# Holding the q attention of a two-layer transformer kernel to a fixed lead over the GLU blocks

## The chip, the cores and the metric

The kernel runs on one core of a Trainium2 chip. A core has five engines that run their own instruction streams and meet at semaphores: TensorE (PE, with its weight loads shown as PEld), VectorE (DVE), ScalarE (ACT), GpSimd (POOL) and SyncE (SP), which in this kernel only issues DMA transfers. The metric is the device time of one execution in microseconds, taken as the median of several runs.

## The reference

The input is 2048 tokens of width 576. Two layers follow each other with the same weights. Each layer adds a linear attention and then a gated unit (GLU) to the residual x, both on a normalised x:

```
x = x + _A_ref(_layernorm(x, axis=-1), A_wqkv, A_w_phi, A_wo)
x = x + _B_ref(_layernorm(x, axis=-1), B_w_gate, B_w_up, B_w_down)

# attention, 32 heads of 18
phi_q = concatenate([softmax(pq), softmax(-pq)])        # pq = q @ w_phi, per head; phi_k likewise
kv  = einsum("bhsf,bhsd->bhfd", phi_k, v)               # sums over ALL tokens
z   = sum of phi_k over the tokens
o   = (phi_q @ kv) / (phi_q @ z + 1e-6),  then o @ wo

# GLU, 4608 hidden columns
h = (x @ w_gate) * (x @ w_up),  then h @ w_down
```

The k side sums over all tokens, so the q side of a layer cannot finish anywhere before the k side has seen every token. After that, each token's q attention and GLU need only that token's data.

## The kernel before, in words

**Tiles and blocks.** The 2048 tokens are 16 tiles of 128 (`NS`), taken in 8 blocks of two tiles (`NB`). The products w_qkv x w_phi for q and k are folded once at the start. The features of phi (2 x 576 = 1152) are handled as nine blocks of 128 (`NK = 9`), so that one DMA transpose turns a tile's phi into nine 128x128 pieces.

**One q tile (`t_aout`).** Ten matmuls with Wq (five per half of 288 columns, L845) go to two PSUM banks. ACT copies them to SBUF (L858), DVE takes maxima and minima (L861, L866), POOL and DVE subtract them (L871, L880), ACT takes exponentials (L888, L890), DVE sums (L895), ACT forms the reciprocal of the sum (L899, L903), and POOL multiplies twice (L909). Lines 849 to 912 are this softmax front. SP then issues the DMA transpose eT<-dd (L1018). Twelve matmuls eT x BD (L1034, called "num" below) give numerators and denominators, DVE divides (L1041 to L1050), SP issues the transpose oT<-o (L1068), ten matmuls with Wo follow (L845 again), and DVE adds the result to x (L1075). When a block's x is complete, its layer norm (`t_ln`) ends in two DMA transposes xT<-xln (L830), which the GLU reads.

**One GLU block (`t_bmain`, `t_down`).** First come 648 matmuls with gate and up weights (L1115). Behind them ACT copies the gate half (L1158) and DVE multiplies (L1160). While they run, the block holds a lock: no other work may take a PSUM bank. Then come 144 down matmuls, 72 of 512 columns (L1182) and 72 of 64 columns (L1185), over 36 chunks of hidden columns. The down weights are not kept: they are loaded again for each block, two chunks (288 KB) at a time, into four slots `wdr` (L1090), on the same SP queue as all transposes. A slot's load can go out once the matmuls on that slot are done.

**k and v of the next layer.** After a GLU block of layer 1 is finished, its two tiles run the k softmax, v and the kv sum of layer 2 (`t_ain`, `t_kv`: matmuls with Wk, Wv and L940).

**What sets the order.** All of this is written as generators ("threads") for a planner (`Sched`, lines 246 to 457). It keeps an estimated time for each engine, takes the request that can start earliest (with a bonus for some priorities), and appends it to its engine's stream. The order of each engine's instructions, SP's included, is thus fixed when the kernel is built; on the chip, each engine takes its own stream in order and waits only for the data and buffers that it needs. An event such as `("x2", L, b)` (GLU block b of layer L is done) orders threads in the planner alone; no wait on the chip comes from it.

**Where the change acts.** `t_q` (line 1224) starts the q attention of a layer, block by block:

```
for b in range(NB):
    yield ("wait", ("xT", L, b))
    if b >= s.pace[L - 1]:
        yield ("wait", ("x2", L, b - s.pace[L - 1]))
    ...
    for j in range(2):
        yield ("go", s.t_aout(L, 2 * b + j), ...)
    ...
    if s.qdeep[L - 1]:
        yield ("wait", ("qf", L, 2 * b + 1))
```

With `pace = (8, 8)` and eight blocks the inner wait is never reached. A second rule works the other way: from block 1 on, GLU block b is not started before the q attention of block b + 1 is finished (`ahead`, line 1313, for `pol = (0, 0)`).

Of the kernel before, what the change touches and what calls it, by code (L numbers as in the profile page):

```python
# [17 lines left out]
class Tracker:  # L18
    def __init__(self):
        self.ops = {e: [] for e in ENGINES}  # L20
        self.count = {e: 0 for e in ENGINES}
        self.know = {e: {} for e in ENGINES}
        self.snap = {}
        self.fin = {}
        self.lastw = {}
        self.readers = {}
        self.lastacc = {}
        self.dma_groups = []
        self.pend_w = {}
        self.pend_r = {}  # L30
        self.stats = {"ops": 0, "waits": 0, "multiwait": 0, "pe_multiwait": 0}
# [479 lines left out]
class K:  # L511
    def __init__(self, nc, A_x, A_wqkv, A_w_phi, A_wo, B_w_gate, B_w_up, B_w_down, out):
        self.nc = nc
        self.A_x, self.A_wqkv, self.A_w_phi, self.A_wo = A_x, A_wqkv, A_w_phi, A_wo
        self.wg, self.wu, self.wd, self.out = B_w_gate, B_w_up, B_w_down, out
        self.NPS, self.NSM, self.NVX, self.NET, self.NXP, self.NWD, self.NG, self.NO, self.NOT = 2, 4, 2, 2, 2, 4, 2, 1, 2
        self.early = 2
        self.qlead = 4
        self.alt = 1.2
        self.lnlead = 9  # L520
        self.pol0 = 1
        self.qdeep = (1, 1)
        self.pol = (0, 0)
        self.pace = (8, 8)
        self.bias = {10: 300.0, 11: 800.0}
        self.tr = Tracker()
        self.sc = Sched(self.tr)
        self.stack = ExitStack()
# [873 lines left out]
```

## Time and profile before

| | |
|---|---|
| median of 3 runs | 1220.92 us (1220.49 to 1225.0) |
| the profiled execution, its own time | 1221.51 us |
| its span, from first to last instruction | 1219.7 us |
| PE busy | 1107.8 us (91%), mean granted clock 0.969 |
| DVE busy | 597.2 us (49%) |
| ACT busy | 390.6 us (32%) |
| POOL busy | 265.0 us (22%) |
| DMA packets of the dynamic queue | 40.2% of 16 engines' span |

The profile is one execution. Its page gives busy times, a chain of work followed back from the last instruction, and groups of instructions with what ended the idle time before them. Other views list the chain in order of time, single stretches of time with each engine's busy time and the granted TensorE clock, and the timeline of one engine. Ends of matmuls are modelled, so the distance between the starts of neighbouring matmuls, not their length, is their cost.

The span divides by PE's work: 0 to 132.3 us is start and the k side of layer 1, and then each layer has eight GLU blocks. A block's gate and up matmuls (L1115) take about 35.5 us. Between them and those of the next block lies a stretch with the down matmuls and with all attention work. These stretches are numbered by layer and block: stretch 1.0 follows the gate and up matmuls of layer 1, block 0, and stretch 2.7 is the last.

### The profile page before, as it was taken

What the parts mean: (1) busy time and instruction counts of PE and PEld (TensorE: products, weight loads), DVE (VectorE), ACT (ScalarE), POOL (GpSimd) and SP (SyncE); (2) the same over time, 40 slices, a digit from 0 to 9 for tenths busy, and PEclk for the clock granted to TensorE, in tenths of its full rate; (3) what the DMA queues carried; (4) which work ended last, traced back from release to release, by engine and by line L of the source; (5) the groups of instructions that cost most, each with busy time, mean ns of one, the idle gap of its engine ahead of it and who ended that gap; (6) DMA issues with size and microseconds to landing.
All of it is one profiled execution on the core that took longest, in us unless ns stands there. A gap on an engine that the chain in (4) does not pass through costs nothing.

```text
span 1219.7 us, 32683 instructions
## 1 busy us (share of the span) xinstructions
PE 1107.8 (91%) x14738; PEld 833.4 (68%) x14806; DVE 597.2 (49%) x1209; ACT 390.6 (32%) x919; POOL 265.0 (22%) x258
## 2 busy tenths in 40 slices
PE   5875898999999999999999589999989999999998
PEld 4553675868768585858586367686766867768684
DVE  7777557384674434343435655737554312223131
ACT  6664433343433232323234343333331212112120
POOL 5674214142250202020203320504221000000000
PEclk9897899999999999999999789999999999999999
DMA  7473119155381605150504211917437152332414
GB/s 178 89 298 96 19 49 212 29 147 108 81 184 13 191 13 175 14 169 21 167 21 145 51 21 41 225 21 194 90 84 177 32 156 69 118 103 85 147 41 146
DMA packets 182949, 128.59 MB, mean 105 GB/s; under 512 B 101530, under 2 KB 181658, under 8 KB 181658
## 3 DMA queue, kind: packets, MB, share of 16 engines
q1 hardware_dynamic: 182810, 126.51, 40.2%
q8 instruction: 115, 1.88, 0.6%
q14 instruction: 24, 0.20, 0.0%
HBM read 100.59 MB, written 2.36 MB: 84 GB/s over the span
## 4 chain that ended last, share of the span: by engine, by line
PE 72%; DMA 15%; DVE 7%; ACT 3%; POOL 1%; issue 1%; SPq 0%; DVEq 0%
PE ps L1115 47%; DMA wdr<-in_B_w_down_dram 11%; PE ps L1182 10%; PE ps L845 10%; DMA oT<-o 3%; PE ps L1185 2%; PE ps L940 1%; POOL dd L909 1%; DVE ss L895 1%; PE ps L1034 1%; DVE st L790 1%; DVE mxmn L866 1%; DVE mxmn L861 1%; ACT dd L888 1%; DVE o L1050 1%
## 5 line engine op out<-in xcount | busy, mean ns | idle before, releaser
L1115 PE MATMUL ps<-xT,Wu 64*128 64x256 bf16 x4608 | 573.4, 270 | 1.2 <-DVE x_sb L1206 0.9
L1115 PE MATMUL ps<-xT,Wg 64*128 64x256 bf16 x4608 | 573.0, 270 | 1.6 <-ACT xT L826 1.6
L1115 PEld LDWEIGHTS ps<-xT,Wg 64*128 64x128 bf16 x4608 | 431.3, 95 | 34.1 <-issue 2.6
L1115 PEld LDWEIGHTS ps<-xT,Wu 64*128 64x128 bf16 x4608 | 434.1, 95 | 29.9 <-DVE x_sb L1206 1.3
L1160 DVE TENSOR_TENSOR hT<-ps,gsb 128x512 bf16<-128x512 f32 x288 | 198.8, 691 | 343.3 <-ACT gsb L1158 342.9
L1158 ACT CAST gsb<-ps 128x512 bf16<-128x512 f32 x288 | 168.4, 585 | 527.4 <-PE ps L1115 526.6
L1182 PE MATMUL ps<-wdr,hT 128*128 128x512 bf16 x1084 | 295.3, 383 | 26.3 <-DMA wdr<-in_B_w_down_dram 25.4
L1182 PEld LDWEIGHTS ps<-wdr,hT 128*128 128x128 bf16 x1152 | 112.8, 98 | 170.2 <-DMA wdr<-in_B_w_down_dram 51.5
L1185 PE MATMUL ps<-wdr,hT 128*128 128x64 bf16 x1152 | 222.6, 193 | 4.6 <-issue 0.8
L1115 PE MATMUL ps<-xT,Wr 64*128 64x256 bf16 x1152 | 171.8, 271 | 0.0
L909 POOL TENSOR_TENSOR dd<-dd,ss 128x576 bf16<-128x576 bf16 x123 | 141.2, 1172 | 137.7 <-ACT ss L903 137.7
L871 POOL TENSOR_TENSOR dd<-psb,mxmn 128x576 bf16<-128x576 bf16 x62 | 72.9, 1180 | 388.9 <-DVE mxmn L861 388.9
L1185 PEld LDWEIGHTS ps<-wdr,hT 128*128 128x128 bf16 x1152 | 113.2, 98 | 1.3
L895 DVE TENSOR_REDUCE ss<-dd 128x64 f32<-128x1152 bf16 x64 | 85.4, 1341 | 32.0 <-ACT dd L890 31.8
L1206 DVE TENSOR_TENSOR x_sb<-ps,x_sb 128x512 bf16<-128x512 f32 x32 | 21.7, 679 | 128.6 <-PE ps L1185 128.6
L812 POOL TENSOR_SCALAR xln<-x_sb,nmean,rstd 128x576 bf16<-128x576 bf16 x59 | 47.9, 820 | 146.3 <-ACT rstd L808 146.3
L1115 PEld LDWEIGHTS ps<-xT,Wr 64*128 64x128 bf16 x1152 | 68.6, 95 | 7.2
L858 ACT CAST psb<-ps 128x288 bf16<-128x288 f32 x128 | 50.0, 396 | 61.1 <-PE ps L845 60.3
L888 ACT ACTIVATE dd<-dd 128x576 bf16<-128x576 bf16 x64 | 43.6, 681 | 63.0 <-DVE dd L880 62.9
L845 PE MATMUL ps<-Wo,oT 128*128 128x288 bf16 x320 | 51.0, 297 | 10.7 <-DMA oT<-o 7.9
L861 DVE TENSOR_REDUCE mxmn<-psb 128x32 f32<-128x576 bf16 x64 | 47.6, 743 | 25.4 <-ACT psb L858 25.4
L845 PE MATMUL ps<-Wv,xT 128*128 128x288 bf16 x320 | 55.0, 307 | 3.7 <-ACT vx L925 2.6
(71 smaller groups left out, 793.1 us busy)
## 6 DMA issues: line engine op xcount, KB each, us to landing
wdr<-in_B_w_down_dram SPq DMA_DIRECT2D x288, 288.0 KB, 3.3
Wg<-in_B_w_gate_dram SPq DMA_DIRECT2D x4, 1152.0 KB, 12.6
Wu<-in_B_w_up_dram SPq DMA_DIRECT2D x4, 1152.0 KB, 14.9
x_sb<-in_A_x_dram SPq DMA_DIRECT2D x8, 288.0 KB, 3.3
out_dram<-x_sb SPq DMA_DIRECT2D x8, 288.0 KB, 3.2
Wraw<-in_A_wqkv_dram SPq DMA_DIRECT2D x8, 144.0 KB, 2.9
xT<-xln SPq DMA_TRANSPOSE x58, 3.1
Wv<-in_A_wqkv_dram SPq DMA_DIRECT2D x1, 576.0 KB, 4.2
```

What stands on the lines that cost most here:

```text
L845: ops.append(Op(d_pe(n), (lambda e, lhsT=lhsT, rhs=rhs, k=k: e.matmul(s.ps[:, bank, 0:n], lhsT, rhs, start=(k == 0), stop=(k == 4))), read ...
L858: yield ("ops", "act", [Op(d_actc(288), (lambda e, h=h, bank=bank: e.copy(psb[:, pz, 288 * h:288 * h + 288], s.ps[:, bank, 0:288])), reads ...
L861: ops = [Op(665, (lambda e: e.tensor_reduce(mxmn[:, pz, 0, :], p3, AX.X, ALU.max)), reads=[("psb", pz, 0), ("psb", pz, 1)], writes=[("mx", ...
L871: yield ("alt", [(eng, [Op(dur, (lambda e: e.tensor_tensor(d1, p3, mxb, ALU.subtract)), reads=[("psb", pz, 0), ("psb", pz, 1), ("mx", pz)] ...
L888: yield ("ops", "act", [Op(590, (lambda e: e.activation(de2, de2, ACTF.Exp, scale=-1.0)), reads=s.ddk(sm, 1), writes=s.ddk(sm, 1))])
L895: Op(1320, (lambda e: e.tensor_reduce(ss[:, sm, :].rearrange("p (b g) -> p b g", b=2), e4, AX.X, ALU.add)), reads=s.ddk(sm, 0) + s.ddk(sm, ...
L909: yield ("alt", [(eng, [Op(dur, (lambda e, ev=ev, rb=rb: e.tensor_tensor(ev, ev, rb, ALU.mult)), reads=s.ddk(sm, br) + [("ss", sm)], write ...
L1115: out.append(Op(54.3, (lambda e, bank=bank, cs=cs, lhsT=lhsT, rhs=rhs, st=st, sp=sp: e.matmul(ps[:, bank, cs], lhsT, rhs, start=st, stop=s ...
L1158: yield ("ops", "act", [Op(540, (lambda e, g=g, gb=gb: e.copy(gsb[:, g, :], ps[:, gb, :])), reads=[("gu", gb)], writes=[("gsb", g)], excl= ...
L1160: yield ("ops", "dve", [Op(625, (lambda e, g=g, ub=ub, p=p: e.tensor_tensor(hT[:, p, :], ps[:, ub, :], gsb[:, g, :], ALU.mult)), reads=[(" ...
L1182: ops.append(Op(d_pe(512), (lambda e, lhsT=lhsT, bank=bank, slot=slot, fi=fi, f=f: e.matmul(ps[:, bank, 0:512], lhsT, s.wdr[:, slot, fi, 0 ...
L1185: ops.append(Op(d_pe(64) + 3, (lambda e, lhsT=lhsT, sl=sl, slot=slot, fi=fi, f=f: e.matmul(ps[:, Z, 64 * sl:64 * sl + 64], lhsT, s.wdr[:, ...
```

## The change

One line: the lead of q attention over finished GLU blocks is limited to 4 blocks in layer 1 and 3 in layer 2.

```diff
@@ -521,7 +521,7 @@
         self.pol0 = 1
         self.qdeep = (1, 1)
         self.pol = (0, 0)
-        self.pace = (8, 8)
+        self.pace = (4, 3)
         self.bias = {10: 300.0, 11: 800.0}
         self.tr = Tracker()
         self.sc = Sched(self.tr)
```

q attention of block b in layer 1 now starts, in the planner, when GLU block b - 4 is done, and in layer 2 when GLU block b - 3 is done. No instruction is added or removed on any engine; their order on all five changes. Matmuls in each stretch, in the order that the two programs have (Wq, Wk, Wv, Wo are L845; num is L1034; kv is L940; all stretches also have the 144 down matmuls):

| stretch | before | after |
|---|---|---|
| 1.0 | num 60, Wq 50, Wo 40 | num 60, Wq 40, Wo 40 |
| 1.1 | Wo 40, num 36, Wq 30, Wk 20, Wv 20, kv 20 | Wo 40, num 36, Wq 20, Wk 20, Wv 20, kv 20 |
| 1.2 | num 60, Wq 40, Wo 40, Wk 20, Wv 20, kv 20 | Wq 20, num 24, Wo 20, Wk 20, Wv 20, kv 20 |
| 1.3 | Wo 20, num 12, Wk 20, Wv 20, kv 20 | the same as 1.2 |
| 1.4 | Wk 20, Wv 20, kv 20 | the same as 1.2 |
| 1.5, 1.6, 1.7 | | as before |
| 2.0 | num 60, Wq 50, Wo 40 | num 48, Wq 20, Wo 40 |
| 2.1 | Wo 45, num 60, Wq 50 | Wq 40, num 24, Wo 20 |
| 2.2 | Wo 55, num 48, Wq 20 | num 24, Wo 20 |
| 2.3 | none | Wq 40, num 24, Wo 20 |
| 2.4 | none | num 24, Wo 20 |
| 2.5 | none | Wq 20, num 24, Wo 20 |
| 2.6, 2.7 | none | none |

In the changed program, PE's order inside the new stretches is (down counts single matmuls):

```
1.2, 1.3, 1.4:  Wq20 down32 Wk5 Wv5 down4 Wk10 Wv5 Wk5 down4 Wv5 down20 Wv5 down8 num12 down20 num12 down16 kv6 Wo5 kv8 Wo5 kv6 down16 Wo5 down4 Wo5 down20
2.1, 2.3:       Wq20 down96 num12 down8 num12 down32 Wo5 down4 Wo5 down4 Wq20 Wo10
2.2, 2.4:       num12 down16 num12 down20 Wo5 down4 Wo5 down16 Wo5 down4 Wo5 down84
```

and SP's order of loads (w) and transposes, where loads of slots 1 to 4 of a stretch have gone out in the stretch before:

```
1.2, 1.3, 1.4:  w5 eT w1 eT w4 oT w3 oT w5 (xT x4 later, beside the gate and up matmuls)
2.1, 2.3:       w8 eT w1 eT w4 oT w4 oT w1 out (xT x2, and eT x2 of the second pair, beside the gate and up matmuls)
2.2, 2.4:       w1 oT w3 oT w8 xT xT w6 out
```

## The prediction

> **What bounds the kernel now.** I read the page's chain first, then the groups, then single stretches. The chain and the costliest down group:
>
> ```profile
> PE 72%; DMA 15%; DVE 7%; ACT 3%; POOL 1%; issue 1%; SPq 0%; DVEq 0%
> ...
> L1182 PE MATMUL ps<-wdr,hT 128*128 128x512 bf16 x1084 | 295.3, 383 | 26.3 <-DMA wdr<-in_B_w_down_dram 25.4
> L1182 PEld LDWEIGHTS ps<-wdr,hT 128*128 128x128 bf16 x1152 | 112.8, 98 | 170.2 <-DMA wdr<-in_B_w_down_dram 51.5
> ```
>
> PE carries the end, and where it does not, a load of down weights does. The same PE work is done after the change, so only PE's idle time and its clock can move. They lie in the stretches between the gate and up matmuls. I asked for these one by one (start:end, then length, then busy time and instructions of PE, PEld, DVE, ACT, POOL, clock, DMA share, GB/s):
>
> ```profile
> 171.10:207.40 36.30, 32.94 (x289) 20.73 (x294) 28.00 (x70) 12.15 (x31) 16.15 (x15) 1.00 0.78 186
> 243.51:279.92 36.41, 34.88 (x305) 22.65 (x310) 30.34 (x71) 15.46 (x43) 18.82 (x18) 1.00 0.64 163
> 315.47:356.64 41.17, 37.37 (x338) 24.88 (x344) 34.60 (x82) 17.15 (x45) 22.06 (x20) 1.00 0.73 169
> 392.19:422.95 30.76, 27.72 (x234) 16.47 (x238) 14.62 (x33) 7.86 (x21) 8.48 (x8) 1.00 0.59 168
> 458.49:485.15 26.66, 24.36 (x202) 13.98 (x206) 10.30 (x18) 7.11 (x17) 6.89 (x6) 1.00 0.58 171
> ...
> 751.10:786.14 35.04, 33.06 (x289) 20.80 (x294) 27.45 (x68) 12.15 (x31) 15.88 (x15) 1.00 0.78 192
> 822.70:859.60 36.90, 32.98 (x294) 21.11 (x299) 29.17 (x74) 13.01 (x35) 16.82 (x16) 1.00 0.85 189
> 895.24:934.41 39.17, 33.36 (x263) 19.83 (x267) 20.85 (x57) 7.37 (x21) 10.10 (x10) 0.91 0.79 178
> 970.00:990.83 20.83, 18.45 (x142) 8.92 (x144) 1.36 (x3) 0.58 (x1) 0.00 (x0) 1.00 0.77 226
> ```
>
> These are stretches 1.0 to 1.4 and 2.0 to 2.3. Even 2.3, with nothing but down matmuls, is not full. The timeline prices PE's work by distance of starts: a pair of down matmuls 0.245 us (402.40 to 402.64), five projections 0.614 (394.61 to 395.22), twelve num 0.62, twenty kv 1.2. So 72 pairs are 17.64 us, and 2.3 holds 3.2 us of **remainder** (length less work). By the same prices the remainders are, from 1.0 to 1.6: 4.5, 2.2, 4.5, 3.9, 2.9, 2.4, 2.0 (22.4 in all), and from 2.0 to 2.6: 3.2, 4.5, 9.8, 3.2, 3.2, 3.2, 2.4 (29.5).
>
> 2.2 stands out. SP's timeline and the chain in order of time show why:
>
> ```profile
> 904.79 3.16 SPq L830 DMA_TRANSPOSE xT<-xln  x2
> 907.99 1.09 SPq L1090 DMA_DIRECT2D wdr<-in_B_w_down_dram  x2
> ...
> 908.62 3.65 DMA wdr<-in_B_w_down_dram
> ```
>
> Two xT transposes, ready only at 904.79, stood ahead of two loads whose slots were free. PE then sat idle for 2.6 us, and the record has PE at half clock for some 3.4 us from 912.2 and again from 929.2 (mean 0.91 in the row above). That is 6.4 us of idle and 3.4 us of lost clock.
>
> **What the skill says.** The Trainium skill, DMA: Bandwidth & Descriptors, "Anatomy of one DMA", has any semaphore wait happen on the issuing sequencer; so one late transpose holds every load behind it. The rows above agree. Its fit there, 2.0 us + bytes/436e3, gives 2.7 us for 288 KB; the trace's median is 3.3, which I use. TensorE: Matmul & The Clock Gate, "Back-to-back issue gap", gives N/2.4 + 2.5 ns: 216 for 512 columns and 29 for 64, in sum 245, as traced. The same page, "What's actually happening", halves the clock after an idle window of about 3.4 us. The trace differs: 2.6 us and 2.2 us of idle were enough, while 2.1 us before 858.9 and 1.7 us before 352.7 were not. So I price idle over 2.2 us in one place at another 1.7 us, half of the time.
>
> **The change part by part.** Nothing is added or removed, and the new condition orders only the planner. No new wait exists on the chip. What changes is the place of each piece, and what stands behind what.
>
> *Layer 1, stretches 1.0 and 1.1.* Each loses ten Wq (1.23 us). 1.0 keeps its other pattern: 36.3 to 35.1. 1.1 has 33.0 us of work and now a longer bare run of down matmuls; with 3.2 of remainder it is 36.2 (before 36.4).
>
> *1.2, 1.3, 1.4.* Each has 80 projections (9.82), num 24 (1.24), kv (1.2) and down (17.64), together 29.9 us. For the remainder I followed one by hand. The first tile's Wq ends at 1.4 us. From there to its eT transpose the trace shows 8.5 to 15.0 us over the tiles in GLU stretches: 12.5 and 13.0 for the pair at 316 us, which k work follows as here, and 15.0 and 14.7 for the pair at 263 us, which is mixed with it. I take 12.5: issue at 13.9. The transpose takes 3.6 to land: 17.5. PE reaches this num after 68 down matmuls and twelve groups of five projections, at 15.9, so it waits 1.6. Then the second eT stands ahead of slot 11's load, and that load comes 1.3 us late. The earlier load holes are filled by Wk and Wv. With slot 10 (0.2) and 0.6 for changing between kinds of matmul (what 2.3 has above the same reckoning) that is 3.7. So 33.6 each, 100.8 for three, against 41.2 + 30.8 + 26.7 = 98.7 before: +2.1. In all layer 1 gives -1.2 - 0.2 + 2.1 = **+0.7**.
>
> *Layer 2, 2.0.* 27.5 us of work and the old 3.2: 30.7 (before 35.0), -4.3.
>
> *2.1 and 2.3.* 60 projections, num 24, down: 26.3 us. The first pair at 751 us, with the same start, issued its eT at 764.62 and 766.36, 13.5 and 15.3 after the stretch began; without the num ahead of it I take 13.0 and 14.7. The 96 down matmuls and two load holes of 0.6 end at 15.6; eT lands at 16.6: 1.0. Slot 13's load stands behind the first eT and slot 14's behind the second: 0.7 and 0.4. With the holes (1.1) and 0.6 for changes the remainder is 3.8: 30.1 each.
>
> *2.2 and 2.4.* 20 projections, num 24, down: 21.3 us. Their q front runs beside the gate and up matmuls, so eT is there at the start. But two xT transposes stand ahead of slot 17. The last Wo ends near 13 us, and in the trace 5.2 to 6.1 us pass from the last addition to x (L1075) to xT; with two issues of 1.25 slot 17 leaves near 21 and lands near 24.5. PE waits about 2.3 there, plus 0.7 at oT, 1.1 at two loads, 0.6: 26.0 each.
>
> *2.5* 23.8 + 3.8: 27.6. *2.6* is as before.
>
> Sum of layer 2: 30.7 - 35.0, 30.1 - 36.9, 26.0 - 39.2, 30.1 - 20.8, 26.0 - 20.9, 27.6 - 20.9 = -4.3 - 6.8 - 13.2 + 9.3 + 5.1 + 6.7 = **-3.2**.
>
> *Gate and up matmuls.* Where Wq groups come just ahead of them, ACT and DVE still have a front to run: 36.6 us after 2.0 before, 35.6 elsewhere. The last Wq group now lies ahead of two such blocks (after 2.1 and 2.3) with two tiles, and no longer ahead of that one. I add 1.0 each and take off 1.2: +0.8; the cover is PSUM's three rotating bank pairs, and without it a whole front on DVE (4.4 us for two tiles) would be the loss. For clock, 2.3 us of idle in 2.2 and 2.4 is at the border: 2 x 1.7 x half = +1.7.
>
> Total: 0.7 - 3.2 + 0.8 + 1.7 = **0.0 us**. The sum is against the profiled execution, 1221.51 (span 1219.7 and 1.8 around it), 0.6 above the median of the runs, 1220.92. I forecast a median of 1221 us, that is, no change.
>
> **The rivals.** A change within 0.5% (6.1 us) can't be told from none.
>
> *Slower: eT comes late in the new stretches.* In seven of them (1.1 to 1.4, 2.1, 2.3, 2.5) the first num and the loads behind the eT wait for a front through ACT, DVE and POOL. For: POOL takes its pieces in order (1.17 us each, seven or more ahead), and the trace has 14.7 to 15.0 us beside k work. Against: 10.3 to 12.1 for pairs alone. Each us beyond what I took is one us per stretch, as no other PE work stands ready. With 15 in four and 13.5 in three it is 4 x 2.5 + 3 x 1.9 = +16, with a clock drop in some: 1237. It decides from 0.9 us late on average (seven stretches, 6.1 us).
>
> *Faster: the spread fills the load holes.* For: 1.4 to 1.6, which have attention and no q front, leave 2.0 to 2.9. If all new stretches left 2.2, layer 1 would gain 3 x 1.5 + 1.0 = 5.5 and layer 2 another 3 x 1.6 + 2 x 2.5 = 9.8, and no clock would drop (1.7): 17 in all, 1204. At half of that, where every new stretch has the 3.2 of bare down matmuls, it is 1212. It decides from 0.7 us less in each of nine. Against: the new 2.1 and 2.3 run 96 down matmuls bare, and the trace has no stretch with a q front below 2.2.
>
> That the change does nothing is excluded: the order differs on all five engines.
>
> **How the numbers follow.** No change 0.45, slower 0.33 (hand reckonings leave out waits for banks and for busy engines, which only add), faster 0.22. The likeliest one's own range is 1215 to 1227. Eight in ten reaches to half of the fast case and to nearly the whole slow one: 1211 to 1236.
>
> **What would show it.** 2.2 at clock 1.00 or shorter than 27 us shows the healed part. 2.1 and 2.3 near 30 and 1.2 to 1.4 near 33 show the remainders; over 32 and 35, with waits for eT and for loads behind it, show the slow rival; under 28.5 and 32, the fast one. The gate and up matmuls after 2.1 and 2.3 should be near 36.6. I am wrong if a clock drop turns up in several new stretches, or if planner and chip disagree on when fronts are ready.

## The result, and the profile after

The changed kernel took 1230.41 us (median of four runs, 1229.0 to 1230.75) against 1222.78 (four runs beside it, 1220.49 to 1225.0): 1.006 of the time before, with a 95% interval of 1.0035 to 1.0086. A second set of runs later gave 1.0051 (1.0033 to 1.0068). So the change costs 0.5 to 0.6%, some 6.1 to 7.6 us. The forecast was 1221, no change; its range, 1211 to 1236, holds the time, but the narrower 1215 to 1227 given for "no change" does not.

The profiled execution of after has a span of 1228.5 us (own time 1230.18), 8.8 above the 1219.7 of before. Its page has the chain and the costliest down group as follows:

```profile
PE 73%; DMA 16%; DVE 4%; ACT 3%; POOL 2%; issue 1%; SPq 0%; DVEq 0%
...
L1182 PE MATMUL ps<-wdr,hT 128*128 128x512 bf16 x1152 | 310.2, 385 | 32.1 <-DMA wdr<-in_B_w_down_dram 31.2
L1182 PEld LDWEIGHTS ps<-wdr,hT 128*128 128x128 bf16 x1152 | 113.5, 98 | 176.2 <-DMA wdr<-in_B_w_down_dram 55.8
```

DMA's share of the chain is one point higher, and the idle time that ends with a load of down weights went from 25.4 to 31.2 us. (The count rises to 1152 because the trace of before lacks some matmul records, not because there is more work.) The view of PE's waits says it more directly. It lists, over the whole span, what PE waited for: us in total, number of times, longest. First before, then after:

```profile
PE ps L1182 <- DMA wdr<-in_B_w_down_dram: 25.4, 46, 2.6
...
PE ps L845 <- DMA oT<-o: 7.9, 10, 2.1
PE ps L1034 <- DMA eT<-dd: 6.7, 1, 6.7
```

```profile
PE ps L1182 <- DMA wdr<-in_B_w_down_dram: 31.2, 48, 2.4
...
PE ps L1034 <- DMA eT<-dd: 10.8, 5, 6.7
PE ps L845 <- DMA oT<-o: 8.2, 9, 2.5
```

Loads cost 5.8 us more and eT transposes 4.1 more. All three rows are transfers that SP issues. (These are single executions: a second profile of the changed kernel, `after_rep`, has 28.8 us of waits for loads and 11.3 for eT.) Where they stand is read from the stretches: 1.0 to 1.4, then 2.0 to 2.5 of after (start:end, length, then busy time and instructions of PE, PEld, DVE, ACT, POOL, then clock, DMA share, GB/s):

```profile
170.54:206.48 35.94, 31.96 (x286) 19.70 (x286) 27.33 (x70) 11.89 (x32) 15.42 (x15) 1.00 0.75 186
242.02:284.04 42.02, 35.59 (x301) 22.54 (x300) 27.21 (x65) 12.94 (x36) 15.72 (x15) 0.96 0.66 142
319.59:351.45 31.86, 30.52 (x269) 19.20 (x270) 23.14 (x50) 11.64 (x30) 13.63 (x12) 1.00 0.66 173
386.99:418.90 31.91, 30.52 (x269) 19.17 (x269) 22.94 (x50) 11.64 (x30) 13.63 (x12) 1.00 0.69 173
454.44:488.90 34.46, 32.08 (x270) 20.01 (x270) 23.28 (x50) 11.63 (x30) 13.63 (x12) 0.95 0.67 161
...
754.67:789.40 34.73, 30.24 (x253) 17.79 (x253) 19.75 (x53) 6.44 (x17) 8.49 (x8) 0.95 0.79 182
824.94:855.15 30.21, 27.36 (x230) 15.82 (x228) 15.45 (x35) 7.21 (x17) 8.02 (x7) 1.00 0.85 217
890.70:916.16 25.46, 22.71 (x190) 12.03 (x190) 7.73 (x23) 1.41 (x5) 1.63 (x2) 1.00 0.81 215
951.70:981.56 29.86, 28.15 (x228) 15.88 (x229) 14.82 (x33) 7.20 (x17) 7.33 (x7) 1.00 0.85 220
1017.20:1044.71 27.51, 24.05 (x189) 12.58 (x190) 7.95 (x23) 1.42 (x5) 1.63 (x2) 0.94 0.83 204
1080.27:1110.46 30.19, 25.64 (x209) 14.06 (x210) 13.98 (x31) 5.61 (x13) 6.86 (x6) 0.99 0.86 217
```

2.2 is healed (25.5 at full clock, before 39.2 at 0.91). But five other stretches now contain or begin 3.4 us of half clock: 1.1, 1.4, 2.0, 2.4 and, at its very end, 2.5. Against before:

| | before | forecast | after | what PE waited for in after (us idle) |
|---|---|---|---|---|
| 1.0 | 36.3 | 35.1 | 35.9 | |
| **1.1** | 36.4 | 36.2 | **42.0** | eT 1.8, load 1.6, oT 2.5; half clock |
| 1.2, 1.3 | 41.2, 30.8 | 33.6 each | 31.9, 31.9 | |
| 1.4 | 26.7 | 33.6 | 34.5 | load 2.1; half clock |
| 1.5, 1.6 | 26.2, 25.8 | as before | 26.7, 26.8 | |
| **2.0** | 35.0 | 30.7 | **34.7** | load 2.4; half clock |
| 2.1, 2.3 | 36.9, 20.8 | 30.1 each | 30.2, 29.9 | |
| 2.2, 2.4 | 39.2, 20.9 | 26.0 each | 25.5, 27.5 | in 2.4 load 2.4; half clock |
| **2.5** | 20.9 | 27.6 | **30.2** | eT 1.4, oT 2.3; half clock behind it |
| 2.6 | 20.0 | as before | 20.4 | |
| sum, layer 1 (1.0 to 1.6) | 223.2 | +0.7 | 229.6 | **+6.4** |
| sum, layer 2 (2.0 to 2.6) | 193.7 | -3.2 | 198.4 | **+4.7** |

The rest of the bridge: the gate and up matmuls are 0.6 shorter in layer 1, and those of block 2.0 are 2.5 shorter, because spells of half clock at the border of the layers fell elsewhere. 6.4 + 4.7 - 0.6 - 2.5 is 8.0 and leaves 0.8 for all other parts: 8.8.

**Stretch 1.1, followed.** POOL's timeline and SP's (start, us, operation, names, count):

```profile
255.49 1.63 POOL L812 TENSOR_SCALAR xln<-x_sb,nmean,rstd 128x576 bf16<-128x576 bf16 x2 [5.56 <-ACT rstd L808]
257.08 4.53 POOL L909 TENSOR_TENSOR dd<-dd,ss 128x576 bf16<-128x576 bf16 x4
```

```profile
257.97 2.53 SPq L830 DMA_TRANSPOSE xT<-xln  x2
260.54 2.95 SPq L1018 DMA_TRANSPOSE eT<-dd  x2
263.54 2.14 SPq L1090 DMA_DIRECT2D wdr<-in_B_w_down_dram  x4
```

The layer norm of block 3 (xln) stands ahead of the softmax's last multiplications on POOL, and its two xT transposes ahead of the two eT on SP. Behind all four stand four loads in a row; the first of them, the one that PE waits for, left 4.6 us after its slot came free. (Lateness of a load is counted here from the last matmul on its slot, less the delay of the quickest loads.) From the tile's last Wq to its eT issue pass 15.1 us; in 1.2 to 1.4, without a norm in between, 10.5. The chain in order of time shows the end of it:

```profile
263.54 3.07 DMA wdr<-in_B_w_down_dram
266.61 0.05 issue
266.65 0.61 PE ps L1182
267.26 0.05 PE ps L1185
...
273.28 5.47 DMA oT<-o
278.75 0.04 issue
278.79 0.79 PE ps L845 x5
```

After 1.8 us of waiting for eT and 1.6 for the load, a pair of down matmuls takes 0.61 + 0.05 and the ones behind it 0.48, where 0.245 is the full-clock price. Then an oT transpose takes 5.5 us to land (median of the 28: 3.4), and PE waits 2.5 more.

**Stretch 2.4.** SP's timeline, then the chain:

```profile
1034.03 2.52 SPq L830 DMA_TRANSPOSE xT<-xln  x2
1036.60 6.66 SPq L1090 DMA_DIRECT2D wdr<-in_B_w_down_dram  x5
```

```profile
1036.60 4.39 DMA wdr<-in_B_w_down_dram
1040.99 0.05 issue
...
1041.90 0.43 PE ps L1182
1042.32 0.05 PE ps L1185
```

Again two xT stand ahead of a load, as in 2.2 before: it left 1.4 us after its slot was free, and landed 4.4 us after its issue (median 3.4). Both parts count. Stretch 2.2 of after has the same order of instructions on PE and SP as 2.4; its load behind the two xT left 1.6 us late, but landed in 3.2 us, and PE waited 1.3 us without a drop of the clock. In 1.4 and 2.0 the loads that PE waited for left 1.7 and 1.0 us late, each behind a single transpose (eT, oT), and took 4.9 and 4.8 us to land. So of these waits a part is order on the SP queue and a part slow landing. Among the loads of after with a transpose in flight beside them 18% took over 4.3 us, among the others 11%; what makes a load land late is not shown.

### The profile page after: what moved, and what is told of

Same layout as the page of the kernel before. It is cut to its first block, busy times and chain, and to the rows that moved or that the text cites. A ratio compares the mean times of both kernels' runs of the same rounds, so it can differ in the third digit from the quotient of the medians.

```text
span 1228.5 us, 32776 instructions
## 1 busy us (share of the span) xinstructions
PE 1111.2 (90%) x14806; PEld 833.7 (68%) x14806; DVE 604.0 (49%) x1209; ACT 389.7 (32%) x919; POOL 265.2 (22%) x258
## 3 DMA queue, kind: packets, MB, share of 16 engines
q1 hardware_dynamic: 182810, 126.51, 41.2%
## 4 chain that ended last, share of the span: by engine, by line
PE 73%; DMA 16%; DVE 4%; ACT 3%; POOL 2%; issue 1%; SPq 0%; DVEq 0%
PE ps L1115 46%; PE ps L1182 12%; DMA wdr<-in_B_w_down_dram 11%; PE ps L845 10%; DMA oT<-o 3%; POOL dd L909 2%; PE ps L1185 2%; PE ps L940 1%; PE ps L1034 1%; DVE ss L895 1%; DMA eT<-dd 1%; ACT dd L888 1%; ACT dd L890 1%; DVE mxmn L866 0%; DVE mxmn L861 0%
## 5 line engine op out<-in xcount | busy, mean ns | idle before, releaser
L1182 PE MATMUL ps<-wdr,hT 128*128 128x512 bf16 x1152 | 310.2, 385 | 32.1 <-DMA wdr<-in_B_w_down_dram 31.2
L1115 PE MATMUL ps<-xT,Wr 64*128 64x256 bf16 x1152 | 162.9, 271 | 0.0
L1115 PEld LDWEIGHTS ps<-xT,Wr 64*128 64x128 bf16 x1152 | 61.2, 95 | 6.9
L861 DVE TENSOR_REDUCE mxmn<-psb 128x32 f32<-128x576 bf16 x64 | 47.7, 745 | 27.8 <-ACT psb L858 27.5
L845 PE MATMUL ps<-Wo,oT 128*128 128x288 bf16 x320 | 50.4, 296 | 10.6 <-DMA oT<-o 8.2
L845 PE MATMUL ps<-Wv,xT 128*128 128x288 bf16 x320 | 54.6, 305 | 4.6 <-ACT vx L925 3.5
```

Source lines behind the costliest of these rows:

```text
L845: ops.append(Op(d_pe(n), (lambda e, lhsT=lhsT, rhs=rhs, k=k: e.matmul(s.ps[:, bank, 0:n], lhsT, rhs, start=(k == 0), stop=(k == 4))), read ...
L1115: out.append(Op(54.3, (lambda e, bank=bank, cs=cs, lhsT=lhsT, rhs=rhs, st=st, sp=sp: e.matmul(ps[:, bank, cs], lhsT, rhs, start=st, stop=s ...
L1182: ops.append(Op(d_pe(512), (lambda e, lhsT=lhsT, bank=bank, slot=slot, fi=fi, f=f: e.matmul(ps[:, bank, 0:512], lhsT, s.wdr[:, slot, fi, 0 ...
```

## The experiments

Theory A, formed from the traces: the loss is made on the SP queue. New pairings of transposes and loads make PE wait for loads, eT and oT, and where a wait is long the clock halves on top. Rival B: the loss comes from PE's new order itself (fewer matmuls standing ready while a front runs), and would be there without any load. Rival C: nearly all of it is clock. (In the recorded expectations "theory B" stands for a loss spread over all new stretches, with no such place, and "theory D" for the cost of the q chain itself or of transposes that come late.)

### Each half of the change alone

```diff
-        self.pace = (4, 3)
+        self.pace = (4, 8)   # layer 1 alone; layer 2 alone: (8, 3)
```

> pace = (4, 8): the layer 1 half of the change alone. Its orders in stretches 1.0 to 1.7 are those of the changed kernel, those of 2.0 to 2.7 are those of the kernel before. Theory A (the loss sits in the stretches where the new order begins, above all 1.1, through transposes ahead of loads on SP and the clock drops that follow): stretch 1.1 near 42 us against 36.4 before, 1.0 to 1.6 together near 229 us against 223; time before + 4 to 8 us, 1227 to 1231. Theory B (the loss is spread over all new stretches alike): 1.1 near 38, the three of 1.2 to 1.4 each 1 to 2 us above 32, time before + 3.

> pace = (8, 3): the layer 2 half alone. Theory A: 2.2 shortened from 39 to about 26 us with the clock at 1.00, but 2.0 at 33 to 35 instead of 35, and 2.3 to 2.5 longer by 25 us in sum, as work moved there; time before + 0 to 5 us, 1222 to 1227, depending on how many clock drops fall. Theory B: before + 5 or more. A part of what the changed kernel gained at the start of layer 2 (2.5 us in the gate and up matmuls of block 2.0) would stay or go with where the clock's windows fall, not with this edit.

Layer 1 alone: 1.0023 of before (1.0009 to 1.0036), 2.9 us where theory A had expected 4 to 8. Layer 2 alone: 1.0035 (1.002 to 1.005). The sum, 0.58%, is what the whole change costs. Each half repeats its stretches: with layer 1 alone 1.1 is 41.1 and 1.4 is 34.4, both with half clock, while 2.2 stays at 40.0; with layer 2 alone 1.1 is 36.2, 2.2 is 25.2, 2.0 is 33.8 and 2.5 is 30.3. So the loss comes from both halves, and the forecast's split by layers (+0.7 and -3.2) failed in both, in layer 2 in sign.

### The same kernel again

> The changed kernel once more, beside the others of this call, for a narrower interval: 5 to 8 us above the kernel before. In the trace, stretch 1.1 again near 42 us or, without a clock drop, near 40; 2.0 again 33 to 35; drops of the clock at other places than in the first profile, since their windows lie elsewhere in each execution.

1.0051 (1.0033 to 1.0068). 1.1 was 40.3, 1.4 34.3, 2.4 26.8, 2.5 30.0, all four with half clock again; 2.0 was 33.4 without. So, against the expectation, most places of half clock belong to the program; whether a given wait tips the clock varies. In 2.2 and 2.4, with one order of instructions, the picture is as in after: the loads left 1.4 us late in both, and landed in 3.0 and 4.3 us.

### Filling the waits

At seven waits of the changed kernel (in 1.1, 1.4, 2.0, 2.4 and 2.5) PE gets 62 extra matmuls whose results nobody uses; at the two waits of 2.2 the kernel before gets 20. The one for down matmuls:

```diff
-        ops = []
+        ops = [Op(0.0, (lambda e: e.matmul(ps[:, Z, 128:512], s.ident[:], s.Wo[:, 0, 0:384], start=False, stop=False, ...)), ...)
+               for _ in range(s.fdown.get((L, b, f), 0))]
```

> The changed kernel with 62 extra matmuls (nothing waits for them, their results are not read) on PE just ahead of the seven instructions that PE waited for longest, 1.0 to 1.6 us of work at each, so that PE is busy through most of these waits. The orders of all other instructions stay. If the half clock after idle is a cause of its own (theory A): no clock drop inside 1.0 to 2.6 at these places, and the time falls by 1.7 us for each of the five drops, to 1221 to 1225. If the drops are only company of the idle and cost nothing more (theory C): 1230 or more, up to 1235 if the extra work isn't hidden.

> The kernel before with 20 extra matmuls ahead of the two instructions of stretch 2.2 that waited 2.6 and 2.2 us for loads. Theory A: the two drops go, 2.2 falls from 39.2 to about 36 us, the time by about 3 us, to 1218 to 1220. Theory C: no change or slower by up to 3 us.

> The kernel before with the 20 extra matmuls ahead of the two waits for loads in stretch 2.2, once more and in more rounds, as it was below both kernels: 0.994 to 0.998 of the kernel before. Stretch 2.2 near 36 us with the clock at 1.00.

The changed kernel filled: 1.0013 of before (0.9999 to 1.0028), 0.4 to 0.5% below the same kernel unfilled. None of the filled places dropped its clock; one new drop stands in 2.6. Stretch 1.1 (row as above):

```profile
243.22:282.54 39.32, 37.82 (x324) 23.79 (x325) 27.16 (x65) 12.93 (x36) 15.72 (x15) 1.00 0.65 150
```

It is 2.7 us shorter than in after, but still 3.1 longer than the forecast: filling removes the half clock and leaves most of the wait. The kernel before, filled, gave 0.9965 (0.995 to 0.998) in six runs and 0.999 (0.9977 to 1.0002) in fourteen; its 2.2 fell from 39.2 to 35.9 and 36.6 at clock 1.00. (The second set missed the expected 0.994 to 0.998; and each profile has one new drop behind stretch 2.1, the first one more in 1.3.) So part of the 0.55% is clock, but the kernel before pays for clock too: filled against filled, 1.0013 to 0.9965 or 0.999, there is still 0.2 to 0.5% left. Rival C alone does not carry the loss; how it splits between clock and waits is not settled closer than that.

### Without the loads

Both kernels with 270 of the 288 loads of down weights left out: after block 0 of layer 1, the down matmuls use what lies in the slots.

```diff
-                yield ("dma", s.g_wd[slot], ...)
+                if (L, b) == (1, 0):
+                    yield ("dma", s.g_wd[slot], ...)
```

> The kernel before without the loads of down weights after layer 1, block 0: the down matmuls of the other blocks read what lies in the four slots, so 270 of 288 loads and their waits are left out and all else stays. It prices all waits for loads: 25 to 45 us less than before, pure down stretches near 18 us instead of 20.9.

> The changed kernel with the same loads left out. Theory A (the loss comes from loads that stand behind transposes on SP): the changed order is no longer behind, -3 to +2 us against the kernel before without these loads. Theory D (PE waits for the q chain itself, for eT and oT with no other work ready): it stays 4 to 8 us behind, with waits for eT and oT in the new stretches.

1181.46 and 1182.46 us: a difference of 1.0 us instead of 6 to 8. With four runs each it is known to some 3.5 us only. PE's waits in the changed kernel without loads (its down matmuls stand one line lower, at L1183):

```profile
PE ps L845 <- DMA oT<-o: 9.8, 10, 1.6
PE ps L1034 <- DMA eT<-dd: 7.2, 2, 6.7
PE ps L1183 <- DMA wdr<-in_B_w_down_dram: 1.1, 3, 0.6
```

The waits for eT are back at 7.2, of which 6.7 is one at the start of a layer's attention that before has too. So beside it PE hardly waits for eT once the loads are gone.

But the pair does not decide between A and B, because PE's order did not stay. The planner, with no loads to place, ordered the rest anew. In the changed kernel 2.0, 2.2 and 2.4 now have 40 Wq each and 2.1, 2.3 and 2.5 none, where after has 20, 0, 0 and 40, 40, 20. In 1.1 the first num stands behind 52 bare down matmuls instead of 32. There eT left nearly as late as in after (14.6 us after its Wq, again behind two xT), and PE did not wait for it: with a later num, the late front cost nothing. Nor do the parts agree as well as the sum: the stretches are still 4.9 us longer in the changed kernel, and the gate and up matmuls 5.3 shorter, because in the kernel before without loads PE waits for DVE in them (3.8 us). What the pair shows is that the shorter lead without loads, in the order that the planner then makes, loses little. It also prices the loads: a stretch of bare down matmuls takes 17.68 us without loads and 20.0 to 20.9 with them, and the kernel before is 40 us shorter.

### The norm in 1.1 put elsewhere

The layer norm of block 3 may use DVE beside POOL, and is transposed by PE and ACT instead of by SP, for this block alone:

```diff
-            yield ("go", s.t_ln([2 * b, 2 * b + 1], [("xTB", L, b)]), 8, ...)
+            yield ("go", s.t_ln([2 * b, 2 * b + 1], [("xTB", L, b)], (L, b) == (1, 3)), 8, ...)
```

> The changed kernel, with the layer norm of layer 1, block 3 done the fast way (normalised on DVE, transposed on PE instead of POOL and SP). That takes two pieces of POOL's work and two xT transposes out of the way of the eT transposes and loads in stretch 1.1; other stretches keep their order. Theory A (1.1 is long because eT came late, behind the layer norm on POOL, and five loads stood behind xT and eT on SP): 1.1 falls from 42.0 to 36 to 38 us, the front from Wq to eT from 15 to about 13, and the time by 3 to 5 us against the changed kernel. Theory B (the length of 1.1 is spread and has no such place): 1.1 stays above 40.

1.0024 (1.0011 to 1.0037), about 0.3% below the changed kernel; 1.1 fell to 39.6. Its row, and SP's timeline there:

```profile
242.25:281.85 39.60, 35.99 (x308) 23.14 (x312) 29.87 (x67) 13.43 (x36) 13.74 (x12) 0.96 0.61 144
```

```profile
258.22 1.34 SPq L1018 DMA_TRANSPOSE eT<-dd  x1
259.61 0.64 SPq L1090 DMA_DIRECT2D wdr<-in_B_w_down_dram  x1
261.23 1.67 SPq L1018 DMA_TRANSPOSE eT<-dd  x1
```

The first eT leaves 12.5 us after its Wq instead of 15.1, and a load now goes between the two. PE's idle time in 1.1 is 3.6 us instead of 6.4. The wait for eT is gone, but half clock remains, a wait of 1.65 us for a load behind the second eT remains, and only about half of the expected gain came. The second eT still took 14.3 us: the norm's work has in part moved to DVE, which the front needs too.

### Loads ahead of transposes

The planner's bonus for priority 3, the loads, is set to 1500 ns: a load that could go within 1.5 us of a transpose goes first.

```diff
-        self.bias = {10: 300.0, 11: 800.0}
+        self.bias = {3: 1500.0, 10: 300.0, 11: 800.0}
```

> The changed kernel with a bonus of 1500 (ns of the planner's time) for the thread that loads down weights, so that on SP a load goes ahead of a transpose which the planner has ready up to 1.5 us earlier. This turns the order on SP round at many places and moves q work too: in layer 2 the first pair of stretches changes places. Theory A (loads behind transposes cost the most): fewer waits for loads of over 1.5 us, time 2 to 6 us below the changed kernel, 1222 to 1226. Theory D (transposes, then late themselves behind loads that wait for their slots, cost as much): within 2 us of the changed kernel or above it.

> The same bonus in the kernel before. Theory A: 2 to 6 us below the kernel before; theory D: within 2 us of it or above.

> The changed kernel with the loads' bias at 1500 again, to see whether the time below both kernels stands. If the first result was the order of the loads: 0.996 to 1.000 of the kernel before, some 0.7% below the changed kernel's 1.005 to 1.006, with 1.1 near 34 us, 2.1, 2.3 and 2.5 at 23 to 27 and 2.2 and 2.4 at 32 to 33. If it was chance of the clock's windows: 1.003 or more.

With the change, 0.998 of before (0.9963 to 0.9997), and when repeated 0.9977 (0.9961 to 0.9992): 0.7 to 0.8% below the changed kernel, and 0.2% below the kernel before. Without the change, 0.9996 (0.998 to 1.0012): nothing. SP in stretch 2.4, and PE's waits, from the repetition:

```profile
1017.28 10.50 SPq L1090 DMA_DIRECT2D wdr<-in_B_w_down_dram  x9
1027.83 1.29 SPq L1018 DMA_TRANSPOSE eT<-dd  x1
1029.16 3.40 SPq L1090 DMA_DIRECT2D wdr<-in_B_w_down_dram  x4
```

```profile
PE ps L1182 <- DMA wdr<-in_B_w_down_dram: 24.5, 44, 2.2
PE ps L845 <- DMA oT<-o: 12.8, 15, 3.0
PE ps L1034 <- DMA eT<-dd: 9.5, 3, 6.7
```

The two eT do not go out in a row, and the loads between them do not wait for the second. Waits for loads are back at the level of before (24.5; after 31.2), paid for with 4.6 us at oT. Of the five half-clock places of after none is left in either profile of this version; a new one stands in 1.0 (41.6 and 40.8 us, where Wo now waits 3 to 4 us), and the first profile has two more, in 1.6 and 2.1, that the second has not. 1.1 is 34.1 and 33.9. In 1.2 to 1.4, where PE's order is that of after but for the place of kv and Wo among the down matmuls, 1.4 lost its wait for a load and its half clock: 32.2 and 32.1 us, where the profiles of after and after_rep have 34.5 and 34.3. In the repetition, the load of slot 11, late in after behind an eT, goes ahead of the second eT here: 0.1 us late and landing in 3.7 us (after: 1.7 and 4.9). In return PE waits 1.3 us for eT. PE's order up to these waits is the same, so this is the cleanest sign that the order on SP counts. For the rest this is not a pure test of the queue, since the planner moved PE's work too: 2.0, 2.2 and 2.4 have 40 Wq each and 2.1, 2.3 and 2.5 none, where after has 20, 0, 0 and 40, 40, 20, and the 20 of 1.1 now lie in 1.0; so 2.2 and 2.4 take 33 us and 2.3 and 2.5 take 24. Nor does the mere number of such pairs decide: a load stands behind two or more transposes in a row in 27 places of before, 20 of after and 12 here; it costs where the slot is free and PE is near. The lateness of loads says the same. Over 0.5 us late are 49 loads in before, 53 in after, 20 and 23 here. In the kernel before with the same bonus only 10 are, and yet its waits for loads are 27.5 us (before 25.4), and it gained nothing. So late loads as such do not make the loss; which ones PE reaches, and how fast they land, decides. The run shows that the shorter lead need not cost anything: with another order of the same instructions it ends below the kernel before. That loads and transposes on SP are the part of the order that counts is shown for 1.4 and fits 1.1; for the whole loss it is argued, since in this run and in the kernels without loads PE's order moved too. Rival B, in the form that PE's order puts a num or a load's matmuls too early for the transfer, stays open.

## Why the prediction missed the direction

**Most of the steps followed by hand came close.** 2.1 and 2.3: forecast 30.1, measured 30.2 and 29.9. 2.2: 26.0, measured 25.5. 1.2 and 1.3: 33.6, measured 31.9, 1.7 us too long each: the front took 10.5 us there, not the 12.5 assumed, and PE did not wait for eT. PE's wait for slot 17's load behind the two xT was put at 2.3 us; it was 2.45 in 2.4 and 1.3 in 2.2, where that load landed in 3.2 us. The load left near 19.5 us in both, not near 21, so in 2.4 a slow landing made up for the earlier start, and the agreement there is in part luck.

**The step that failed is "1.1 has 33.0 us of work ... with 3.2 of remainder" and "2.0 ... 27.5 us of work and the old 3.2".** These two stretches, at the seam where the new order begins, were not followed; they got remainders from other stretches. Their remainders are 9.0 and 7.2. That is 5.8 + 4.0 = 9.8 us, more than the whole loss. The trace of before had what was needed for 1.1: the prediction itself quotes fronts of 14.7 to 15.0 us where k work is mixed in, and kept this for the slow rival; the new front took 15.1. For 2.0, SP's timeline and the chain of after:

```profile
775.75 1.20 SPq L1068 DMA_TRANSPOSE oT<-o  x1
776.99 0.58 SPq L1090 DMA_DIRECT2D wdr<-in_B_w_down_dram  x1
777.62 2.52 SPq L830 DMA_TRANSPOSE xT<-xln  x2
...
776.99 4.82 DMA wdr<-in_B_w_down_dram
```

A load left 1.0 us late behind an oT, with two xT right after it, and took 4.8 us to land; PE waited 2.4 us for it and the clock halved. In the two profiles after_rep and l2only PE waited here for the next load, behind the two xT, for 2.1 and 2.4 us. None of this was in the borrowed remainder.

**Two terms were mis-sized.** 2.5 was given 3.8 of remainder and has 6.4: its first eT landed after 5.6 us (forecast 3.6), and its last oT (4.0) ended with no down matmul left to run beside it. 1.4 is 0.9 over, and 1.5 and 1.6, taken as unchanged, gave 1.5 together.

**The clock was foreseen in kind, not in number.** Two border cases at half chance made +1.7. There were five (before: two in stretches). "I am wrong if a clock drop turns up in several new stretches" is what happened. Of the two named, 2.4 dropped and 2.2 did not; 1.1, 1.4, 2.0 and 2.5 had waits of over 2 us that the reckoning did not contain. The price of one, 1.7 us, was about right. In eleven of the twelve sets of twelve and more runs the times fall by 0.6 to 1.1 us per 0.001 of mean granted clock (in the twelfth by 0.15), and 3.4 us at half clock are 0.0014 of it: an estimate of 0.9 to 1.6 us.

**Gate and up matmuls** after 2.1 and 2.3 took 35.5 and 35.6 us, not 36.6: PE waited for nothing there. The one block that is longer, after 2.5 (36.8), runs its first part at half clock.

**The rivals.** The slow one named the right sign and nearly the right waits, but mostly the wrong places: eT late in seven stretches. In six of them it was issued earlier than forecast (10.3 to 11.8 us after its Wq), and only 1.1 had the 15 us that the rival put on four stretches; of the loads behind an eT, the one in 1.4 came late. The fast rival was right for 1.2 and 1.3 (31.9), but 1.1 alone used up that gain.

**Luck.** That the wide range holds the time is no credit to the mechanism: it was made to reach over most of the slow rival. The waits at the seam were left out, and the gains that did come, 1.7 us each in 1.2 and 1.3 and 2.5 in the gate and up matmuls of 2.0, were not forecast either; without these 5.9 us the time would have stood at the range's end.

## What to carry to other kernels

When work is spread over stages, follow by hand the stages at the seam, where old and new order meet; a remainder borrowed from another stage is worth nothing there. Where loads and dependent transposes share one issuing queue, look at the neighbours in that queue: a load whose buffer is free can stand behind a transpose, and it costs where PE reaches that load soon after. A change that removes such a stall in one place can set one up in another. Look at the landing time as well as the issue: here it made the difference between 2.2 and 2.4. Judge a spread and the queue's order together: here the spread alone lost 0.5%, the loads' priority alone gave nothing, and both together gained 0.2%.

## What the runs showed of the hardware

The clock follows a fixed grid, which decides whether a wait of about 2 us costs another microsecond or two. In after, the half-clock spells begin at 266.54, 474.75, 781.95, 1041.36 and 1109.63 us; the distances are 61, 90, 76 and 20 times 3.4133 us, to within 0.01. The Trainium skill, TensorE: Matmul & The Clock Gate, "What's actually happening", says as much (a free-running window of 3413 ns) and has the clock halve after a window of idle. The runs differ on how much idle that takes. I summed PE's idle time (by the modelled ends of matmuls) in each grid window at full clock, from 170 us on, over the twelve profiles with all loads in place: of 50 windows with more than 2.05 us of idle, every one was followed by half clock; of some 3500 with less than 1.73, none; of the 26 between, 12. So in these runs the limit lay between 51 and 60% of a window, split or in one piece. This accounts for the drop in 1.1: 1.8 us and 1.6 us of idle stand close together there, with 2.6 us in one window, while 2.5 us before the Wo at 278.79, of which the grid put 2.0 into one window, did not. By the same count a single wait between 2 and 2.5 us can tip the clock in one execution and not in another, as the grid cuts it: 2.0 had half clock in after and none with layer 2 alone, after one wait of 2.4 us in each.
